# Probability rows in explicitly chosen unit slots, earlier VectorE exponentials, and background matmuls in steps of two, in a fused attention and GLU block

## The chip, the cores and the metric

The kernel runs on one core of one Trainium2 chip. The metric is the device time of one execution in microseconds (us). Executions of one kernel on one chip mostly agree within 1%. "Span" is the length of the profiled execution from its first to its last instruction; it is 1.8 to 2.0 us shorter than the time of the same execution. The profiled execution of the kernel before took 901.75 us, some 4 us less than the median of its runs in the tables, so leads against its profile come out about that much smaller than the differences of medians.

## The reference

One transformer block on 2048 rows of width 512 in bf16: 32 heads of width 16, then a gated MLP of width 1792.

```python
x = A_x                                               # 1 x 2048 x 512
h = x + _A_ref(_layernorm(x), A_wqkv, A_wo)           # softmax attention, 32 heads
h2 = h + _B_ref(_layernorm(h), B_w_gate, B_w_up, B_w_down)
# _A_ref: scores = q k^T * 16**-0.5; p = softmax(scores); o = p v; o @ wo
# _B_ref: (sigmoid(x @ w_gate) * (x @ w_up)) @ w_down
```

The attention makes 32 x 2048 x 2048 exponentials. The kernel cuts them into 2048 **units** of 128 keys x 512 queries of one head (written 128x512 in the profile).

## The kernel before

TensorE makes score tiles in PSUM (transposed: keys on partitions). ScalarE turns most units into fp16 probabilities with `Exp` (`pt`). VectorE makes the others with integer tricks: one instruction per unit from PSUM (`J`), then, for four units together, two bit operations and two products (`X`), which it does in a `chain` of deferred pieces. TensorE multiplies the probabilities with the values into one PSUM accumulator (`acc`), for four heads (a *group*) at a time; at the end of a group VectorE takes `acc` out, and only then the next group's products may start. Normalisation, the Q, K and V projections, the output projection and the MLP of query chunks that are done run as *background* between these.

All order is decided when the program is built: Python keeps a modelled time of each engine (`T["P"]`, `T["A"]`, `T["D"]`) and emits each engine's instructions in the order that the model gives. The pieces that the change touches (cuts are marked `...`):

```python
ptp = main.enter_context(tc.tile_pool(name="ptp", bufs=7))   # 7 tiles of GU = 3 units
NPT = 7

def flush():                     # emit EVERY VectorE and ScalarE job that is ready
    ...
def force(tag):                  # tag: something a score or value matmul needs now
    while After(tag).end is None:
        flush()
        if After(tag).end is None:
            try_bg(1e9, 1e12)

def prep_v(t):                   # one background item: V of 128 keys
    yield pe(4, pm_new)          # ask for room for 4 matmuls at once
    ps = pm_tile()
    v_mm(ps, t)
    done["v", t] = [pm_out(dve(603, lambda: v_out(ps, t), st["mark"]))]

def pt_tile(n):
    if wide["n"] == GU:
        return ptp.tile([P, GU, QC], FP16, name="pt")[:]
    ...                          # early: two-unit places in X, J and 7 "hold" tiles

while n + 1 < len(tiles):        # one exp tile per turn
    ...
    if wide["n"] < GU and not early_on and wide["base"] == 4:   # from 2 to 3 units a tile
        flush()
        wide.update(n=GU, base=2)
    pss_n[n + 1] = scores(n + 1)
    ...
    dable = (len(tl) == GU and tl[-1][:2] not in ((0, 0), (0, 1)) and ...)
    split = (dable and max(T["D"], ...) <= start + 600 and ...)  # last unit to VectorE?
    wa = len(tl) - split
    pt = pt_tile(n)
    ex = nc.scalar.activation(out=pt[:, 0:wa, :], in_=pss[:, 0:wa, :], func=ACT.Exp, scale=AS)
    if split:
        dexp_first(pss[:, GU - 1, :], tl[-1], n)                 # VectorE's J
    ...                          # then background and value matmuls until the exp ends
```

A tile usually gives one of its three units to VectorE, so that seven tiles of three hold about 16 units (in the trace 488 exps from `pt` tiles make two units and 174 make three).

Of the kernel before, what the change touches and what calls it, by code (L numbers as in the profile page):

```python
# [10 lines left out]
FP16 = mybir.dt.float16  # L11
BF16 = mybir.dt.bfloat16
# [131 lines left out]
def kernel(  # L144
# [41 lines left out]
    otp = main.enter_context(tc.tile_pool(name="otp", bufs=6))  # L186
    ptp = main.enter_context(tc.tile_pool(name="ptp", bufs=7))
    dvx = main.enter_context(tc.tile_pool(name="dvx", bufs=1))
# [353 lines left out]
    def prep_v(t):  # L542
        yield pe(4, pm_new)
        ps = pm_tile()
        v_mm(ps, t)
        done["v", t] = [pm_out(dve(603, lambda: v_out(ps, t), st["mark"]))]

    def early_ln(c):
        pr = c
        js = []  # L550
        for i in range(TQ):
            j = None
            if tasks["s", c, i].end is None:
                j = dve(810, lambda i=i: ln_stats(xb[c][:, i, :], mvs[c][:, i, :]), pr=pr)
            elif tasks["f", c, i].end is None:
                j = dve(150, lambda i=i: fix(c, i), pr=pr)
            js.append(j)
        jn = newton_jobs(rstds[c][:], mvs[c][:, :, 1], *js, pr=pr)
        ja = []
        for i in range(TQ):  # L560
            ja.append(dve(325, lambda i=i: apply(c, i), jn, After(("x", c - 1, i // 2)), pr=pr))

        def turn():
            for i in range(0, TQ, 2):
                yield pe(4, pm_new, ja[i], ja[i + 1], ns=8 * 75.0)
                ps = pm_tile()
                pt = ps.bitcast(BF16).rearrange("p (i b q) -> p i b q", i=2, b=DC)
                for k in range(2):
                    for b in range(DC):
                        nc.tensor.transpose(out=pt[:, k, b, :],  # L570
                                            in_=buf["xn", c, i + k][:, b * P:(b + 1) * P],
                                            identity=ident_bf[:])
                pm_out(dve(605, lambda i=i, pt=pt: nc.vector.tensor_copy(
                    out=xnT[c][:, :, i * P:(i + 2) * P].rearrange("p b (i q) -> p i b q", i=2),
                    in_=pt), st["mark"]))
                done["x", c, i // 2] = [st["pms"][-1]]
        return turn()
# [10 lines left out]
    def prep_k(p):  # L588
        for c in range(NQC):
            yield pe(4, pm_new)  # L590
            ps = pm_tile()
            proj8(ps, wk_sb, p, c)
            done["k", p] = [pm_out(dve(603, lambda ps=ps, c=c: nc.vector.tensor_copy(
                out=KT[p][:, c * QC:(c + 1) * QC], in_=ps), st["mark"]))]

    def prep_q(qc, p):
        yield pe(4, pm_new)
        ps = pm_tile()
        proj8(ps, wq_sb, p, qc)
        qd = work.tile([P, QC], BF16, name="qd", bufs=2)  # L600
# [47 lines left out]
    def wo_ln(qc):  # L648
# [5 lines left out]
        for i in range(TQ):  # L654
            yield pe(4, pm_new, otj[qc, NP - 1])
            ps = pm_tile()
            wo_mm(ps, qc, i)

# [26 lines left out]

    def gate_mm(ps, w):
        for d in range(DC):
            nc.tensor.matmul(ps, lhsT=w[:, d, :], rhs=hnT[:, d, :],  # L688
# [34 lines left out]
    def ffn_up(qc, f):  # L723
        yield pe(4, pm_new)
        if f == 0:
# [4 lines left out]
        ps = pm_tile()  # L730
        gate_mm(ps, wgu[:, 0])
        ja = pm_out(act(478, lambda: th.update({f: tanh_out(ps)}), st["mark"]))
        yield pe(4, pm_new)
        ps2 = pm_tile()
        gate_mm(ps2, wgu[:, 1])
        if f % 2:
# [7 lines left out]
    def ffn_down(qc, i):  # L744
        hT, ps = hts[qc], None
        for f in range(0, FC, 4):
            n = min(4, FC - f)
            if f:
# [44 lines left out]
    def try_bg(tokens, loose=60.0, depth=1):  # L793
# [15 lines left out]
        return mm  # L809

    def force(tag):
        while After(tag).end is None:
            flush()
            if After(tag).end is None:
                try_bg(1e9, 1e12)

# [17 lines left out]
    N = ahead // GU  # L834
    wide = {"n": 2, "base": 4}
    STAGES = (150, 225, 360, 530)
# [47 lines left out]
    def scores(n):  # L884
# [4 lines left out]
        pss = PS[:, base:base + wide["n"], :]  # L889
        wide["base"] = {(2, 4): 6, (2, 6): 4, (3, 2): 5, (3, 5): 2}[wide["n"], base]  # L890
        for ui, (qc, g, kt, j) in enumerate(tiles[n]):
# [10 lines left out]
    class Unit:  # L902
        def __init__(self, u, ap, n, end):
            self.u, self.ap, self.n, self.end, self.d = u, ap, n, end, -1

    avq = []
    av_end = {}
    count, todo = {}, {}
    for qc, g in gseq:
        for j in range(4):  # L910
            count[qc, g, j], todo[qc, g, j] = 0, NT
    NPT = 7

    def finish_group(qc, g):
# [52 lines left out]
    def av(limit, loose=60.0):  # L967
# [20 lines left out]
        for un in uns:  # L988
            if un.d < 0:
                av_end[un.n] = T["P"] + DRAIN  # L990
        qc, g = uns[0].u[:2]
# [9 lines left out]
    def dexp_first(src, u, n):  # L1001
# [9 lines left out]
        uns = [Unit(u, None, n, None) for s in range(2)]  # L1011
        for un in uns:
            un.d = 1
        avq.extend(uns)
# [43 lines left out]
    def want_dve(n):  # L1058

        quads[:] = [q for q in quads if any(un in avq for un in q)]  # L1060
        if wide["n"] < GU or not blocks or any(un.n in hold for un in avq):
            return False
# [8 lines left out]

    slots, hold = [], {}

    def early_slots():
        for name, b in (("X", XB), ("J", JB)):
            for i in range(b):
                x = dvx.tile([P, 2, 4, QC] if name == "X" else [P, 4, QC], I16, name=name, bufs=b)
                for s in range(2):
                    slots.extend(([x[:, s, 0:2, :], x[:, s, 2:4, :]]) if name == "X" else [x[:, 2 * s:2 * s + 2, :]])
        slots.extend(prep.tile([P, 2, QC], I16, name=f"hold{i}")[:] for i in range(7))  # L1080

    def pt_tile(n):
        if wide["n"] == GU:
            return ptp.tile([P, GU, QC], FP16, name="pt")[:]
        if not slots:
            early_slots()
        while True:
            busy = {hold[un.n] for un in avq if un.n in hold}
            s = next((s for s in range(len(slots)) if s not in busy), None)
            if s is not None:  # L1090
                break
            flush()
            if not av(8, 1e12):
                try_bg(1e9, 1e12)
        hold[n] = s
        return slots[s].bitcast(FP16)

# [20 lines left out]
    while n + 1 < len(tiles):  # L1118
# [3 lines left out]
        early_on = any(b[1][0] in EARLY for b in bg)  # L1122
        if wide["n"] < GU and not early_on and wide["base"] == 4:
            flush()
            wide.update(n=GU, base=2)
            st["R"] = 1
            N = n + 2 + -(-sum(b.left() for b in blocks) // GU)
        if blocks:
            pss_n[n + 1] = scores(n + 1)
        pss = pss_n.pop(n)  # L1130
        while any(un.n <= n - NPT and un.d < 0 and un.n not in hold for un in avq):
            flush()
            if av(8, 1e12):
                continue
            if half and not chain:
                dexp_rest()
            if not chain:
                break
            pop_chain()
        start = max(T["A"], sc_end[n] + LAT)  # L1140
        if n - NPT not in hold:
            start = max(start, av_end.get(n - NPT, 0.0) + LAT)
        busy = sum(j.ns for j in dq if j.ready() is not None)
        pend = sum(c[0] for c in chain)
        dable = (len(tl) == GU and tl[-1][:2] not in ((0, 0), (0, 1))
                 and not any(un.n in hold for un in avq))
        split = (dable and max(T["D"], sc_end[n] + LAT) <= start + 600 and (half or (len(quads) < XB and len(open_j) < JB))
# [5 lines left out]
        wa = len(tl) - split  # L1153
        pt = pt_tile(n)
        ex = nc.scalar.activation(out=pt[:, 0:wa, :], in_=pss[:, 0:wa, :], func=ACT.Exp, scale=AS)  # L1155
        T["A"] = start + 51 + 426.5 * wa
        ex_end[n] = T["A"] + TAIL["A"]
        avq.extend(Unit(u, pt[:, ui, :], n, ex_end[n]) for ui, u in enumerate(tl[:wa]))
        if split:
            dexp_first(pss[:, GU - 1, :], tl[-1], n)  # L1160
            ex_end[n] = max(ex_end[n], T["D"] + TAIL["D"])
# [24 lines left out]
        if tl[0][0] == NQC - 1 and tiles[n - 1][0][0] < NQC - 1:  # L1186
            nc.sync.dma_start(out=xl[:], in_=x_v[:, (NQC - 1) * TQ:NQC * TQ, :])
        if fw is None and After(("q", 0, NP - 1)).end is not None:
            pre.close()
            fw = main.enter_context(tc.tile_pool(name="fw", bufs=1, reuse_waits="tile"))  # L1190
# [81 lines left out]
    for k, i in enumerate(order):  # L1272
        hn = hnl[i] = ptp.tile([P, GU, QC], FP16, name="pt")[:, 0, :].bitcast(BF16)
        if k % 2 == 0:
# [77 lines left out]
```

## Time and profile before

| | before |
|---|---|
| time, median of 4 runs | 906.2 us (905.28 to 907.01) |
| ScalarE / VectorE / TensorE busy | 86% / 88% / 85% of the span |
| exp units by ScalarE / VectorE | 1561 / 487 |
| first VectorE exp starts | 94.6 us |

The view of busy time by stretches of the kernel before, for the start (17 to 94 us), two parts of the attention and the end. Its columns are the stretch and its length, busy time and number of instructions of TensorE, of TensorE's weight loads, of VectorE (DVE), ScalarE (ACT) and GpSimd, the granted TensorE clock, DMA share and GB/s.

```profile
core 0: us, PE busy (x) PEld busy (x) DVE busy (x) ACT busy (x) POOL busy (x), PEclk, DMA share, GB/s
17.00:94.00 77.00, 57.52 (x396) 19.96 (x397) 39.58 (x102) 57.74 (x54) 0.00 (x0) 0.87 0.08 25
110.00:330.00 220.00, 178.37 (x1393) 50.75 (x1393) 211.83 (x386) 202.91 (x196) 0.00 (x0) 0.91 0.03 8
330.00:800.00 470.00, 423.93 (x3190) 122.01 (x3189) 454.30 (x817) 427.82 (x434) 0.00 (x0) 0.96 0.09 28
840.00:900.00 60.00, 51.18 (x254) 22.09 (x254) 24.82 (x48) 22.02 (x36) 0.00 (x0) 0.95 0.24 74
```

From 330 to 800 us VectorE is 97% busy and ScalarE 91%. At the start VectorE works only half of the time.

ScalarE's waits of the kernel before (who waited for whom; total us, times, longest us). L985 is the value matmul, L893 the score matmul:

```profile
ACT pt L1155 <- PE PS L985: 38.6, 26, 5.2
ACT pt L1155 <- PE PS L893: 19.2, 33, 1.8
ACT th L716 <- PE PS L688: 18.8, 16, 2.1
ACT X L1155 <- PE PS L893: 17.2, 7, 14.4
```

An exp that waits for a *value* matmul doesn't lack input; it lacks a free place to write, since the matmul that still has to read the old contents of its slot has not run. That is 38.6 us. An exp that waits for a *score* matmul lacks input.

The longest slot wait, in the timeline of the kernel before (start, length, engine, line, what; in brackets the idle time before it and who ended it):

```profile
490.80 1.06 PE L893 MATMUL PS<-QT_90,KT_85 32*128 32x512 bf16 x6
491.14 0.54 DVE L674 TENSOR_SCALAR hn<-h,mv,rstd 128x512 bf16<-128x512 f32 x1
...
492.39 0.56 DVE L1033 TENSOR_SCALAR X<-J 128x1536 int16<-128x1536 int16 x1
492.86 1.02 DVE L1043 TENSOR_TENSOR X<-J,X 128x1024 f16<-128x1024 f16 x2
493.00 1.52 PE L985 MATMUL PS<-X,Vaug 128*17 128x512 f16 x6 [1.15 <-DVE X L1033]
494.56 0.72 DVE L940 STREAM_TRANSPOSE xs<-PS 128x512 f32<-128x512 f32 x1 [0.68 <-PE PS L985]
...
495.33 1.03 PE L985 MATMUL PS<-pt,Vaug 128*17 128x512 f16 x8 [0.81 <-DVE xs L940]
...
496.01 4.43 ACT L1155 ACTIVATE pt<-PS 128x1536 f16<-128x1536 f32 x4 [5.16 <-PE PS L985]
```

Read it backwards: ScalarE starts at 496.0 because value matmuls of the next group (495.3) have freed a slot. Those waited for the accumulator's transpose (494.6), this for the last value matmuls of the old group (493.0), and these for VectorE's last `X` pieces (492.4), which stood behind other jobs in VectorE's order. TensorE's scores for the next tiles were done at 491.9, but all seven tiles were full of the next group's probabilities.

The start of the kernel before, in its timeline:

```profile
26.44 0.40 PE L570 MATMUL PS<-ident_bf,xn_336 128*128 128x128 bf16 x4 [0.89 <-DVE xn_336 L328]
...
30.89 0.69 DVE L237 BATCH_NORM_STATS2 st<-xb_111 128x6 f32<-128x512 bf16 x1
...
36.30 0.68 DVE L573 COPY xnT_81<-PS 128x1024 bf16<-128x1024 bf16 x1
...
37.03 1.87 PE L583 MATMUL PS<-xnT_81,w_114 128*128 128x512 bf16 x4 [10.20 <-DVE xnT_81 L573]
...
40.33 1.94 ACT L1155 ACTIVATE X<-PS 128x1024 f16<-128x1024 f32 x2 [14.42 <-PE PS L893]
```

The transposes of key chunk 1 are done at 26.8 us; VectorE copies them out (`xnT_81`) only at 36.3, after statistics of chunk 3 (`xb_111`) that nobody needed yet. ScalarE idles 14.4 us.

### The profile page before, as it was taken

How to read it: one execution, taken by the hardware profiler on the slowest of the kernel's cores; microseconds unless marked ns; L12 is line 12 of the kernel's file. 1: busy time of each engine (PE TensorE's matmuls, PEld its weight loads, DVE VectorE, ACT ScalarE, POOL GpSimd, SP SyncE). 2: the span in 40 equal slices, each digit the busy share in tenths (PEclk: the TensorE clock that was granted, in tenths of full speed). 3: DMA queues.
4: the chain of work that ended last, by engine and by line, in shares of the span. 5: the costliest groups of instructions: out<-in, count | busy, mean ns of one | idle time of the engine just before them, and what ended most of it. 6: DMA issues, size and time to landing. Idle time of an engine off the chain costs nothing.

```text
span 900.0 us, 14693 instructions
## 1 busy us (share of the span) xinstructions
PE 765.6 (85%) x5644; PEld 232.0 (26%) x5644; DVE 795.4 (88%) x1470; ACT 770.8 (86%) x783; POOL 2.9 (0%) x7
## 2 busy tenths in 40 slices
PE   4498888877787899999998989989978898989897
PEld 2132222222222222222222222222222222222343
DVE  7742899999999899999998999999999999899832
ACT  5399998989989999999898999988898998899741
POOL 1000000000000000000000000000000000000000
PEclk9699998899988999999997899999998999899999
DMA  5020002000000001111000001110100101000500
GB/s 198 1 83 1 1 1 59 1 1 2 1 1 1 13 1 47 49 50 33 19 19 1 24 24 48 42 42 13 36 13 1 47 25 34 15 1 13 170 7 27
DMA packets 38219, 26.16 MB, mean 29 GB/s; under 512 B 2560, under 2 KB 38144, under 8 KB 38144
## 3 DMA queue, kind: packets, MB, share of 16 engines
q1 hardware_dynamic: 36512, 23.99, 8.7%
q10 hardware_dynamic: 1632, 1.18, 0.4%
q8 instruction: 46, 0.75, 0.4%
q14 instruction: 29, 0.24, 0.1%
HBM read 23.07 MB, written 2.10 MB: 28 GB/s over the span
## 4 chain that ended last, share of the span: by engine, by line
DVE 37%; ACT 26%; PE 23%; issue 12%; DMA 0%; ACTq 0%; DVEq 0%
ACT pt L1155 23%; DVE J L1007 15%; DVE X L1043 7%; PE PS L688 6%; PE PS L985 5%; PE PS L893 5%; DVE X L1033 4%; DVE X L1038 3%; DVE xs L940 2%; PE PS L264 1%; DVE hT L700 1%; PE PS L1298 1%; PE PS L259 1%; PE PS L705 1%; ACT th L716 1%
## 5 line engine op out<-in xcount | busy, mean ns | idle before, releaser
L1155 ACT ACTIVATE pt<-PS 128x1024 f16<-128x1024 f32 (+1 forms) x663 | 700.8, 1169 | 60.3 <-PE PS L985 38.6
L1007 DVE TENSOR_SCALAR J<-PS 128x512 int16<-128x512 f32 x487 | 324.6, 685 | 16.2 <-PE PS L893 9.1
L985 PE MATMUL PS<-pt,Vaug 128*17 128x512 f16 x1499 | 218.4, 406 | 7.0 <-DVE xs L940 6.8
L1043 DVE TENSOR_TENSOR X<-J,X 128x1024 f16<-128x1024 f16 (+1 forms) x251 | 161.7, 669 | 0.0
L985 PE MATMUL PS<-X,Vaug 128*17 128x512 f16 x1014 | 150.9, 396 | 6.5 <-DVE X L1033 4.7
L985 PEld LDWEIGHTS <-Vaug 128*17 128x17 bf16 x2535 | 63.6, 89 | 151.5 <-issue 130.3
L688 PE MATMUL PS<-xnT_80,wgu 128*128 128x512 bf16 x336 | 89.3, 389 | 1.2 <-DVE hT L700 0.8
L1038 DVE TENSOR_SCALAR X<-J 128x2048 int16<-128x2048 int16 (+3 forms) x133 | 85.3, 642 | 0.2
L1033 DVE TENSOR_SCALAR X<-J 128x2048 int16<-128x2048 int16 (+3 forms) x133 | 85.2, 640 | 0.0
L700 DVE SCALAR_TENSOR_TENSOR hT<-th,PS 128x512 bf16<-128x512 f32 x56 | 38.2, 681 | 18.8 <-PE PS L688 18.8
L716 ACT ACTIVATE th<-PS 128x512 f32<-128x512 f32 x56 | 34.8, 621 | 18.8 <-PE PS L688 18.8
L893 PE MATMUL PS<-QT_90,KT_85 32*128 32x512 bf16 x256 | 39.5, 428 | 12.5 <-ACT pt L1155 12.0
L893 PE MATMUL PS<-QT_93,KT_86 32*128 32x512 bf16 x256 | 37.8, 397 | 10.1 <-ACT pt L1155 9.5
L893 PE MATMUL PS<-QT_92,KT_86 32*128 32x512 bf16 x256 | 37.2, 381 | 10.4 <-ACT pt L1155 9.9
L893 PE MATMUL PS<-QT_91,KT_85 32*128 32x512 bf16 x256 | 36.4, 395 | 11.1 <-ACT pt L1155 10.5
L893 PE MATMUL PS<-QT_94,KT_87 32*128 32x512 bf16 x256 | 35.4, 384 | 11.3 <-ACT pt L1155 11.0
L893 PEld LDWEIGHTS <-KT_84 32*128 32x128 bf16 x512 | 20.5, 91 | 92.0 <-issue 87.3
L705 PE MATMUL PS<-wd,hT 128*128 128x512 bf16 x168 | 43.9, 382 | 0.4 <-DVE ob L710 0.4
L893 PE MATMUL PS<-QT_95,KT_87 32*128 32x512 bf16 x256 | 37.0, 392 | 8.0 <-ACT pt L1155 7.6
L893 PEld LDWEIGHTS <-KT_85 32*128 32x128 bf16 x512 | 20.4, 92 | 89.4 <-issue 88.1
L893 PEld LDWEIGHTS <-KT_86 32*128 32x128 bf16 x512 | 20.2, 91 | 84.7 <-issue 84.4
L893 PEld LDWEIGHTS <-KT_87 32*128 32x128 bf16 x512 | 19.4, 91 | 84.2 <-issue 83.2
(220 smaller groups left out, 531.1 us busy)
## 6 DMA issues: line engine op xcount, KB each, us to landing
wgu<-in_B_w_gate_dram SPq DMA_DIRECT2D x21, 256.0 KB, 2.8
wgu<-in_B_w_up_dram SPq DMA_DIRECT2D x21, 256.0 KB, 3.2
out_dram<-ob SPq DMA_DIRECT2D x16, 128.0 KB, 1.7
wd<-in_B_w_down_dram SPq DMA_DIRECT2D x1, 1792.0 KB, 7.2
xr<-in_A_x_dram SPq DMA_DIRECT2D x12, 128.0 KB, 2.7
X<-in_B_w_gate_dram SPq DMA_DIRECT2D x3, 512.0 KB, 3.9
X<-in_B_w_up_dram SPq DMA_DIRECT2D x3, 512.0 KB, 4.9
wv_sb<-in_A_wqkv_dram SPq DMA_DIRECT2D x1, 512.0 KB, 6.2
```

Source lines behind the costliest of these rows:

```text
L688: nc.tensor.matmul(ps, lhsT=w[:, d, :], rhs=hnT[:, d, :], start=(d == 0), stop=(d == DC - 1))
L700: nc.vector.scalar_tensor_tensor(out=hT[:, f, :], in0=th[:], scalar=1.0, in1=ps, op0=ALU.add, op1=ALU.mult)
L705: nc.tensor.matmul(ps, lhsT=hT[:, f, i * P:(i + 1) * P], rhs=wd[:, f, :], start=(f == 0), stop=(f == FC - 1))
L716: nc.scalar.activation(out=th[:], in_=ps, func=ACT.Tanh, scale=0.5)
L893: mm = nc.tensor.matmul(pss[:, ui, :], lhsT=KT[g // 2][32 * j:32 * j + 32, kt * P:(kt + 1) * P], rhs=q[32 * j:32 * j + 32, :], start=True, ...
L940: j = st["acc"] = dve(650, lambda: nc.vector.transpose(out=xs[:].rearrange("p b r -> p (b r)"), in_=acc), Mark(T["P"] + DRAIN), pr=-1)
L985: nc.tensor.matmul(acc[32 * j:32 * j + VW, :], lhsT=Vaug[:, kt, h, :], rhs=un.ap, start=(c == 0), stop=(todo[qc, g, j] == 0), tile_positio ...
L1007: nc.vector.tensor_scalar(out=J[:, k, :], in0=src, scalar1=ZOFF, scalar2=0.0, op0=ALU.add, op1=ALU.max)
L1033: V.tensor_scalar(out=X[:, 0, 0:k, :], in0=J[:, 0:k, :], scalar1=POWER, scalar2=LITTLE, op0=ALU.bitwise_and, op1=ALU.bitwise_or)
L1038: V.tensor_scalar(out=X[:, 1, 0:k, :], in0=J[:, 0:k, :], scalar1=FRACTION, scalar2=HALF, op0=ALU.bitwise_and, op1=ALU.bitwise_or)
L1043: V.tensor_tensor(out=x, in0=J[:, a:b, :].bitcast(FP16), in1=x, op=ALU.mult)
L1155: ex = nc.scalar.activation(out=pt[:, 0:wa, :], in_=pss[:, 0:wa, :], func=ACT.Exp, scale=AS)
```

## The change

Its intent: (1) probability rows live in unit slots, 36 in one tile and 14 more while the preparation lasts; each exp takes the run of free slots whose last reader is modelled to be done first; (2) `force` emits only the jobs that the wanted result depends on, and normalisation jobs of later chunks come after V's casts; (3) VectorE may take units much earlier; the width of exp tiles goes from 2 to 3 in stages; (4) background matmuls ask for room two at a time. The core of the diff, cuts marked:

```diff
-    ptp = main.enter_context(tc.tile_pool(name="ptp", bufs=7))
+    ptp = main.enter_context(tc.tile_pool(name="ptp", bufs=1))
...
     def prep_v(t):
-        yield pe(4, pm_new)
+        yield pe(2, pm_new, After(("x", t // TQ, t % TQ // 2)))
         ps = pm_tile()
-        v_mm(ps, t)
-        done["v", t] = [pm_out(dve(603, lambda: v_out(ps, t), st["mark"]))]
+        v_mm(ps, t, 0, 2)
+        yield pe(2)
+        v_mm(ps, t, 2, 4)
+        done["v", t] = [pm_out(dve(603, lambda: v_out(ps, t), st["mark"], pr=1))]
...  (the same split for K, Q, the output projection, gate, up and down)
     def early_ln(c):
-        pr = c
+        pr = 2 * (c - 1)
...
+    def place_now(job):
+        if isinstance(job, After):
+            for j in done.get(job.tag, ()):
+                place_now(j)
+        elif isinstance(job, Later):
+            place_now(job.job)
+        elif isinstance(job, Job) and job.end is None:
+            for d in job.deps:
+                place_now(d)
+            if job.ready() is not None:
+                q, e = (dq, "D") if job in dq else (aq, "A")
+                q.remove(job)
+                job.place(e)
+
     def force(tag):
         while After(tag).end is None:
-            flush()
-            if After(tag).end is None:
-                try_bg(1e9, 1e12)
+            place_now(After(tag))
+            if After(tag).end is None and not try_bg(1e9, 1e12):
+                for d in bg[0][2][2]:
+                    place_now(d() if callable(d) else d)
...
+    PLACES = {3: ((4, 2), (6, 2)), 2: ((3, 3), (6, 2)), 1: ((2, 3), (5, 3))}
+    WHEN = {"d": ("k0", 1), 2: ("k0", 2), 1: ("v", NT - 1)}
...
-        if wide["n"] < GU or not blocks or any(un.n in hold for un in avq):
+        if not blocks or not late("d"):
             return False
...
+    NPT, NPE = 36, 14
+    PT = ptp.tile([P, NPT, QC], FP16, name="pt")
+    PE_ = prep.tile([P, NPE, QC], FP16, name="pe")
...
-        dable = (len(tl) == GU and tl[-1][:2] not in ((0, 0), (0, 1))
-                 and not any(un.n in hold for un in avq))
+        dable = len(tl) > 1 and busy <= 1500
...
-        pt = pt_tile(n)
-        ex = nc.scalar.activation(out=pt[:, 0:wa, :], in_=pss[:, 0:wa, :], func=ACT.Exp, scale=AS)
+        free_at, row = p_slots(wa)
+        pt = row[0].tile[:, row[0].i:row[0].i + wa, :]
+        ex = nc.scalar.activation(out=pt, in_=pss[:, 0:wa, :], func=ACT.Exp, scale=AS)
```

## The prediction

> **What bounds the kernel now.** In the middle VectorE and ScalarE share the exponentials, and both are nearly full: the view of busy time by stretches gives, for 300 to 400 us, VectorE 98%, ScalarE 96%, TensorE 90%. Over 100 to 840 us VectorE is idle about 4%, ScalarE about 8%. TensorE has slack: in the list of waits its score matmuls wait 82 us for ScalarE to empty PSUM. One exp unit (128x512) costs ScalarE about 0.46 us, VectorE about 1.35 us (657 us in four groups of lines, 487 units). The middle makes about 2.6 units per us.
>
> Two kinds of time are lost.
>
> 1. The start. The timeline shows ScalarE idle 14.4 us (25.9 to 40.3); it waits for the scores of key chunk 1. VectorE is busy in that gap with statistics and Newton steps of chunks 2 and 3, while the second copy of chunk 1's transposes starts at 36.3, 9.5 us after they ended: `force` flushes every ready job ahead of the needed one. TensorE is idle 10.2 us as well and its clock falls to 0.5, so four dense matmuls take 1.87 us, not 1.04. The Trainium skill ("TensorE: Matmul & The Clock Gate", "What's actually happening") says an idle array runs at half rate; the trace agrees (only 0.5 or 1.0). From 50 to 94 us VectorE is busy 14 to 58%; its first exp comes at 94.6 us.
>
> 2. ScalarE waits for probability slots: 38.6 us in 26 waits for the value matmuls (longest 5.2 us, in a half-clock stretch), I think mostly where one head group ends and the next one's probabilities pile up. Seven tiles hold about 16 units at the usual two per tile.
>
> **What the change does.**
> - `place_now` and the new priorities put only chunk 1's chain on VectorE. By its durations (Newton 2.2 us, four applies 1.3, two copies 1.4, projection 1 to 1.9, cast 0.7) K of chunk 1 is there at 25 to 27 us. The gap shrinks to 0 to 3 us: gain 11 to 13 us, fully critical.
> - VectorE exps from the second chunk on: until about 54 us its fixed work nearly fills it; then some 20 us of idle become about 14 units: gain 4 to 6 us.
> - 36 slots, no longer in threes, hold over twice the units. Slot waits fall from 38.6 us to 5 to 12. Some 28 us of ScalarE are 60 units, over 2.6 per us 23 us; part turns into waits for scores: 12 to 22 us.
> - Steps of two cost TensorE switches: four dense matmuls take 0.97 us from start to next start where 4 x 0.216 is 0.86, so about 0.1 us for each of about 190 split pieces, at most 19 us, against 82 us of slack: off the path, and the next scores come sooner. Net zero to 3 us gained.
> - The last 60 us don't change.
>
> Sum: 27 to 44 us, discounted for overlap. Predicted: 872 us, range 856 to 889. Chances: faster by over 2% 0.83, within 2% 0.15, slower by over 2% 0.02.
>
> **What would show it.** The ScalarE gap near 26 us is under 3 us; the first VectorE exp comes before 60 us; ScalarE's waits for value matmuls total under 15 us; in 100 to 800 us ScalarE is over 94% busy; VectorE makes 495 to 540 units; from the last exp to the end stays near 57 us.
>
> **What would make it wrong.** TensorE becomes the limit (ScalarE's waits for scores rise above the 19 us of now, or more half-clock stretches); early VectorE exps delay V and K casts and stall TensorE; regions of one large tile bring false waits; VectorE at 98% is already the limit.

## The result

| | before | after |
|---|---|---|
| time, median of 4 runs | 906.2 us | 864.65 us (862.06 to 865.35) |
| ratio | | 0.9537 (95%: 0.9514 to 0.9559) |
| ScalarE / VectorE / TensorE busy | 86 / 88 / 85% | 89 / 91 / 88% |
| units by ScalarE / VectorE | 1561 / 487 | 1567 / 481 |
| half-clock time, 110 to 330 us | 41.0 us | 78.5 us |

A ratio is the mean time of one kernel's runs over that of the other kernel's runs of the same rounds, so it isn't quite the ratio of the medians in the tables. Half-clock time is added up from the trace's record of the granted clock, in time from the start of the span (the record begins about 16 us into it).

The stretches of the kernel after (the last one starts where its last exp unit ends):

```profile
core 0: us, PE busy (x) PEld busy (x) DVE busy (x) ACT busy (x) POOL busy (x), PEclk, DMA share, GB/s
17.00:94.00 77.00, 65.03 (x451) 19.96 (x451) 65.83 (x152) 57.64 (x62) 0.00 (x0) 0.91 0.07 25
110.00:330.00 220.00, 179.90 (x1353) 46.73 (x1351) 202.16 (x367) 200.48 (x191) 0.00 (x0) 0.82 0.03 8
330.00:800.00 470.00, 440.40 (x3426) 123.48 (x3424) 459.02 (x828) 462.96 (x466) 0.00 (x0) 0.98 0.10 29
806.00:863.00 57.00, 48.47 (x231) 21.17 (x228) 21.68 (x43) 17.78 (x31) 0.00 (x0) 0.97 0.20 63
```

Three things stand out. From 330 to 800 us ScalarE rose from 427.82 of 470 us (91%) to 462.96 (98.5%). From 110 to 330 us it did not rise at all, and the clock fell from 0.91 to 0.82. And from 17 to 94 us ScalarE was busy about as long as before (57.64 against 57.74 us), although the gap that the change aimed at is closed.

ScalarE's waits of the kernel after (L1016 is now the value matmul, L927 the score matmul):

```profile
ACT pt L1181 <- PE PS L927: 37.2, 35, 9.7
ACT th L724 <- PE PS L696: 14.9, 14, 1.1
...
ACT pt L1181 <- PE PS L1016: 3.8, 3, 1.7
```

The slot waits fell from 38.6 to 3.8 us. The waits for scores total about what they were (19.2 and 17.2 before, 37.2 now), with a new longest of 9.7 us.

The start of the kernel after, in its timeline:

```profile
25.62 1.02 PE L585 MATMUL PS<-xnT_81,w_114 128*128 128x512 bf16 x4 [0.93 <-DVE xnT_81 L575]
...
27.86 9.27 ACT L1181 ACTIVATE pt<-PS 128x1024 f16<-128x1024 f32 x10 [2.78 <-PE PS L927]
...
37.74 0.68 DVE L1038 TENSOR_SCALAR J<-PS 128x512 int16<-128x512 f32 x1
...
46.73 1.33 DVE L1038 TENSOR_SCALAR J<-PS 128x512 int16<-128x512 f32 x2
...
49.04 0.68 DVE L237 BATCH_NORM_STATS2 st<-xb_111 128x6 f32<-128x512 bf16 x1
...
55.70 1.87 PE L585 MATMUL PS<-xnT_83,w_114 128*128 128x512 bf16 x4 [0.78 <-DVE xnT_83 L575]
...
59.05 1.94 ACT L1181 ACTIVATE pt<-PS 128x1536 f16<-128x1536 f32 x2 [9.72 <-PE PS L927]
```

The gap before chunk 1 shrank from 14.4 to 2.8 us. VectorE's first exp starts at 37.7 us. But the last statistics of chunk 3 (`xb_111`) run at 49.0 us, behind VectorE exps (`J`), and ScalarE then idles 9.7 us for the keys of chunk 3. The four matmuls at 55.7 run at half clock (1.87 us instead of 1.02).

To see where time is won I count, in each trace, the exp units that are done (columns of each ScalarE exp / 512, plus one for each `J`), and note when the n-th is reached. This "unit curve" is worked out from the trace's instructions and is used for all runs below. It rests on one profiled execution of each kernel:

| units done | before, us | after, us | lead, us |
|---|---|---|---|
| 32 | 49.7 | 35.3 | 14.4 |
| 64 | 66.6 | 60.5 | 6.1 |
| 192 | 118.6 | 109.7 | 8.9 |
| 512 | 237.8 | 234.2 | 3.6 |
| 1024 | 433.4 | 428.3 | 5.1 |
| 1536 | 640.1 | 619.3 | 20.8 |
| 2048 | 844.1 | 805.9 | 38.3 |
| end of span | 900.0 | 863.3 | 36.7 |

The lead of 14 us at the start is mostly gone at once, and 33 of the 38 us come in the second half of the units.

### The profile page after: what moved, and what is told of

The parts are those of the page before. It is cut to its first block, busy times and chain, and to the rows that moved or that the text cites. A ratio compares the mean times of both kernels' runs of the same rounds, so it can differ in the third digit from the quotient of the medians.

```text
span 863.3 us, 14366 instructions
## 1 busy us (share of the span) xinstructions
PE 759.1 (88%) x5638; PEld 219.8 (25%) x5638; DVE 781.3 (91%) x1450; ACT 768.2 (89%) x783; POOL 2.9 (0%) x7
## 4 chain that ended last, share of the span: by engine, by line
ACT 38%; PE 34%; DVE 19%; issue 8%; DMA 1%; SPq 0%; DVEq 0%; ACTq 0%
ACT pt L1181 35%; PE PS L1016 10%; PE PS L927 9%; PE PS L696 7%; DVE J L1038 7%; DVE X L1072 3%; PE PS L713 2%; DVE X L1062 2%; DVE X L1067 2%; PE PS L1331 1%; DVE hT L708 1%; PE PS L259 1%; ACT th L724 1%; PE PS L264 1%; ACT pe L1181 1%
## 5 line engine op out<-in xcount | busy, mean ns | idle before, releaser
L1181 ACT ACTIVATE pt<-PS 128x1024 f16<-128x1024 f32 (+2 forms) x670 | 706.6, 1184 | 43.2 <-PE PS L927 37.2
L1038 DVE TENSOR_SCALAR J<-PS 128x512 int16<-128x512 f32 x481 | 317.6, 681 | 26.9 <-PE PS L927 19.1
L1016 PE MATMUL PS<-pt,Vaug 128*17 128x512 f16 x1515 | 210.2, 409 | 1.0 <-DVE nt L631 0.3
L1072 DVE TENSOR_TENSOR X<-J,X 128x1024 f16<-128x1024 f16 (+1 forms) x247 | 158.8, 665 | 0.0
L1016 PE MATMUL PS<-X,Vaug 128*17 128x512 f16 x962 | 148.3, 402 | 6.0 <-DVE X L1062 4.1
L696 PE MATMUL PS<-xnT_80,wgu 128*128 128x512 bf16 x336 | 94.0, 384 | 3.2 <-DVE hT L708 2.2
L1016 PEld LDWEIGHTS <-Vaug 128*17 128x17 bf16 x2529 | 60.7, 90 | 139.9 <-issue 118.8
L1067 DVE TENSOR_SCALAR X<-J 128x2048 int16<-128x2048 int16 (+2 forms) x128 | 83.1, 650 | 0.1
L1062 DVE TENSOR_SCALAR X<-J 128x2048 int16<-128x2048 int16 (+2 forms) x128 | 82.9, 647 | 0.0
L927 PE MATMUL PS<-QT_91,KT_85 32*128 32x512 bf16 x256 | 39.7, 437 | 11.1 <-ACT pt L1181 10.6
L927 PE MATMUL PS<-QT_90,KT_85 32*128 32x512 bf16 x256 | 39.4, 434 | 11.0 <-ACT pt L1181 10.6
L713 PE MATMUL PS<-wd,hT 128*128 128x512 bf16 x168 | 47.5, 383 | 0.3 <-DVE ob L718 0.2
L927 PE MATMUL PS<-QT_92,KT_86 32*128 32x512 bf16 x256 | 38.5, 410 | 8.3 <-ACT pt L1181 7.8
L927 PE MATMUL PS<-QT_95,KT_87 32*128 32x512 bf16 x256 | 38.1, 392 | 6.8 <-ACT pt L1181 6.1
L927 PEld LDWEIGHTS <-KT_85 32*128 32x128 bf16 x512 | 19.8, 93 | 93.2 <-issue 91.9
L927 PEld LDWEIGHTS <-KT_84 32*128 32x128 bf16 x512 | 20.2, 91 | 90.7 <-issue 85.0
L927 PE MATMUL PS<-QT_93,KT_86 32*128 32x512 bf16 x256 | 36.6, 394 | 6.8 <-ACT pt L1181 6.3
L927 PEld LDWEIGHTS <-KT_86 32*128 32x128 bf16 x512 | 19.1, 91 | 83.2 <-issue 82.7
L927 PE MATMUL PS<-QT_94,KT_87 32*128 32x512 bf16 x256 | 36.3, 382 | 4.3 <-ACT pt L1181 4.0
L927 PEld LDWEIGHTS <-KT_87 32*128 32x128 bf16 x512 | 19.5, 91 | 79.1 <-issue 78.1
```

What stands on the lines that cost most here:

```text
L696: nc.tensor.matmul(ps, lhsT=w[:, d, :], rhs=hnT[:, d, :], start=(d == 0), stop=(d == DC - 1))
L713: nc.tensor.matmul(ps, lhsT=hT[:, f, i * P:(i + 1) * P], rhs=wd[:, f, :], start=(f == 0), stop=(f == FC - 1))
L927: mm = nc.tensor.matmul(pss[:, ui, :], lhsT=KT[g // 2][32 * j:32 * j + 32, kt * P:(kt + 1) * P], rhs=q[32 * j:32 * j + 32, :], start=True, ...
L1016: nc.tensor.matmul(acc[32 * j:32 * j + VW, :], lhsT=Vaug[:, kt, h, :], rhs=un.ap, start=(c == 0), stop=(todo[qc, g, j] == 0), tile_positio ...
L1038: nc.vector.tensor_scalar(out=J[:, k, :], in0=src, scalar1=ZOFF, scalar2=0.0, op0=ALU.add, op1=ALU.max)
L1062: V.tensor_scalar(out=X[:, 0, 0:k, :], in0=J[:, 0:k, :], scalar1=POWER, scalar2=LITTLE, op0=ALU.bitwise_and, op1=ALU.bitwise_or)
```

## The experiments

Twelve kernels ran, all correct. Their ratios against the kernel before, each measured on the same chip in the same rounds:

| run | what | median, us | ratio (95%) | lead at unit 1024 / 2048, us |
|---|---|---|---|---|
| after | the change | 864.65 | 0.9537 (0.9514 to 0.9559) | 5.1 / 38.3 |
| closed | change + guard (control) | 869.55 | 0.9611 (0.9584 to 0.9638) | 8.9 / 33.5 |
| dlate3 | change, wish for VectorE later | 869.72 | 0.9621 (0.9586 to 0.9656) | 9.0 / 35.3 |
| steps4 | change, steps of four | 879.59 | 0.9723 (0.9687 to 0.9760) | 7.7 / 34.2 |
| slots21 | change, 21 slots | 879.17 | 0.9727 (0.9693 to 0.9761) | 2.9 / 25.0 |
| slots15 | control, 15 slots | 901.20 | 0.9951 (0.9915 to 0.9988) | -4.8 / 3.8 |
| before_pt12 | before, 12 tiles | 867.64 | 0.9603 (0.9569 to 0.9638) | 7.2 / 37.6 |
| before_force | before, forcing by need | 881.66 | 0.9758 (0.9716 to 0.9800) | 3.8 / 21.7 |
| dgate3 | control, VectorE units from chunk 3 | 853.24 | 0.9429 (0.9401 to 0.9458) | 21.7 / 52.5 |
| fill2 | control + useless matmuls | 851.38 | 0.9404 (0.9360 to 0.9449) | 17.0 / 49.1 |
| fill2_dry | fill2's order without them | 861.98 | 0.9550 (0.9507 to 0.9593) | 10.5 / 41.4 |
| gatefill | dgate3 + fill2 | 845.23 | 0.9341 (0.9292 to 0.9389) | 23.6 / 55.9 |
| gatefill_all | the same, fillers everywhere | 839.60 | 0.9293 (0.9245 to 0.9341) | 26.5 / 62.4 |

One caution for reading it: the order is chaotic. `after`, `closed` and `dlate3` differ by edits that should change little, yet they spread from 0.9537 to 0.9621. Differences under about 1% between kernels whose order was reshuffled are not laid to a cause here. The unit curve has scatter of its own: fill2 and fill2_dry (below) give the engines the same work up to the first useless matmul at 140 us, and yet their profiles reach unit 64 at 64.5 and 60.1 us, with 17.1 and 10.2 us of half clock in the first 110 us. Differences of some 4 us between two curves are therefore not read as effects.

### Steps of four in the changed kernel (steps4)

```diff
-        yield pe(2, pm_new)
+        yield pe(4, pm_new)
...  (all seven kinds of background matmul, undone as in the kernel before)
```

> The kernel after with the background matmuls in steps of four again (V, K, Q, output projection, gate, up, down); slots, early units and forcing as in the change. Facts of the two traces: the change's lead over before is 14 us at the 32nd exp unit, 5 us at the 1024th, 38 us at the 2048th, so nearly all is won in the second half, where the FFN's background runs. Theory 1 (deeper slots won the second half): total within 8 us of after (857 to 873 us), lead at unit 2048 over 30 us. Theory 2 (the steps of two won it): 880 us or more, ScalarE's waits for scores in 430 to 800 us come back.

Measured: 879.59 us; lead at unit 2048 34.2 us. Neither theory as put: the exps end only 4 us later than in after (810.0 against 805.9 us), but the end is 11.4 us longer (from unit 2048 to the end of the span 68.8 us, after 57.4, before 55.8). The timeline of TensorE in this run shows why: three down-projection tiles of the MLP were left over when the exps were done and ran alone (after has none of these three there).

```profile
813.75 3.18 PE L705 MATMUL PS<-wd,hT 128*128 128x512 bf16 x14 [1.55 <-DVE hT L700]
817.71 3.18 PE L705 MATMUL PS<-wd,hT 128*128 128x512 bf16 x14 [0.78 <-DVE ob L710]
821.67 3.18 PE L705 MATMUL PS<-wd,hT 128*128 128x512 bf16 x14 [0.78 <-DVE ob L710]
825.33 0.39 PE L1255 MATMUL PS<-xnT,ident 128*128 128x512 bf16 x1
```

So in the changed kernel some 11 us of what the steps of two bring are background work that is not left over. That room for four matmuls at once is found too seldom is the likely reason; it was not counted. In before_pt12 steps of four left far less over (58.7 us from unit 2048 to the end), so this holds for this order, not in general.

### 21 slots in the changed kernel (slots21)

```diff
-    NPT, NPE = 36, 14
+    NPT, NPE = 21, 14
```

> The kernel after with 21 unit slots in the main tile instead of 36 (the bytes of the seven tiles of before; the 14 early slots stay). Theory 1 (depth of the slots): 880 to 900 us, ScalarE again waits over 20 us for value matmuls. Theory 2 (steps of two): 857 to 872 us. A middle result, 870 to 880, would mean that both are needed or that 21 single slots already hold more than seven tiles used at two units each.

Measured: 879.17 us, the middle result; ScalarE waits 22.7 us for value matmuls, where after has 3.8 us:

```profile
ACT pt L1181 <- PE PS L1016: 22.7, 17, 2.6
```

It loses 11 us against after between units 1024 and 2048. Depth matters, but this alone doesn't say how much, since 21 single slots already hold more than 7 tiles at two units each.

### A later wish for VectorE units (dlate3)

```diff
-    WHEN = {"d": ("k0", 1), 2: ("k0", 2), 1: ("v", NT - 1)}
+    WHEN = {"d": ("k0", 3), 2: ("k0", 2), 1: ("v", NT - 1)}
```

> The kernel after with VectorE units allowed from the 4th key chunk on instead of the 2nd. In after's trace the last statistics of chunk 3 run only at 49 us, behind VectorE exps, and ScalarE then idles 9.7 us for that chunk's keys. Theory A (early exps delay the chunk-3 chain): the 9.7 us gap shrinks below 4 us and the total falls by 2 to 8 us against after. Rival B (the gap comes from the order of the normalisation jobs alone): the gap stays above 7 us and the total is the same or up to 4 us longer, since units move from VectorE to ScalarE.

Measured: 869.72 us, gap still 9.73 us. This decides nothing, and the reason is a flaw of the experiment: in its trace VectorE's exps still begin at 39.5 us. `want_dve` only chooses which unit stands last in a tile; whether VectorE takes it is decided by `dable`, which the change freed of any condition on the stage. That reading of the code led to dgate3.

### Twelve tiles in the kernel before (before_pt12)

```diff
-    ptp = main.enter_context(tc.tile_pool(name="ptp", bufs=7))
+    ptp = main.enter_context(tc.tile_pool(name="ptp", bufs=12))
...
-    NPT = 7
+    NPT = 12
```

> The kernel before with 12 probability tiles of three units (36 units) instead of 7, nothing else. Theory 1 (depth of the slots): 870 to 888 us, ScalarE's 38.6 us of waits for value matmuls fall under 12 us. Theory 2 (steps of two): the slot waits fall too but turn into waits for scores, 893 to 906 us.

Measured: 867.64 us, ratio 0.9603. Theory 1 holds, and the run is 2.4 us faster than its range: two changed numbers in the program give 36.5 us (medians 904.1 and 867.64). ScalarE's waits in this run (the last line has the slot waits):

```profile
ACT X L1155 <- PE PS L893: 17.2, 7, 14.4
ACT th L716 <- PE PS L688: 14.7, 13, 1.1
ACT pt L1155 <- PE PS L893: 13.9, 30, 1.8
...
ACT pt L1155 <- PE PS L985: 4.3, 3, 1.7
```

The slot waits did not turn into waits for scores: those fell too, from 19.2 to 13.9 us. The 14.4 us gap at the start is still there; the lead is -0.8 us at unit 192, 7.2 us at 1024 and 37.6 us at 2048. Busy time moved as a slot story wants it: from 330 to 800 us ScalarE rose from 427.82 to 461.19 us. The Trainium skill ("Perfetto Trace Analysis", "Optimization Strategy") says that consistent bubbles on the engine that should be saturated can mean that there isn't enough SBUF or PSUM for the next tile; this agrees, with 26 such bubbles of 38.6 us cut to 3 of 4.3 us by buffer count alone.

### The control (closed)

While I prepared variants with another order, some were refused before any run, because a PSUM bank was read in the middle of an accumulation: with steps of two, another background item can begin between the halves of one, or the number of banks can change there. The control adds a guard:

```diff
+            if oi is not None and bg[i] is not oi:      # a half-done tile goes first
+                continue
...
-        if st["R"] > 1 and wide["i"] == 0 and late(st["R"] - 1):
+        if st["R"] > 1 and wide["i"] == 0 and not st["open"] and late(st["R"] - 1):
```

> Control. The kernel after with a guard only: while a background tile has had two of its four matmuls, no other background tile is begun, and the number of banks is not changed. Variants of the change with another order of work were refused without it (a bank was read in the middle of an accumulation). It changes a few positions in the order. Expected: after's time within the scatter that a reshuffled order brings, 860 to 872 us, same unit curve within 4 us; the next three runs are compared with this one.

Measured: 869.55 us, within what was expected. It is the measure for the next runs.

### Fifteen slots (slots15)

```diff
-    NPT, NPE = 36, 14
+    NPT, NPE = 15, 14
```

> The control with 15 unit slots in the main tile, which is what seven tiles hold at two units each, so before's effective depth, with all else of the change kept. Theory 1 (depth of the slots carries the gain, 36.5 us in the run of the kernel before with twelve tiles): 888 to 905 us, ScalarE's waits for value matmuls 30 us or more. Theory 2 (early units, forcing and steps of two carry a good half): 875 to 887 us. With 21 slots it was 879 us.

Measured: 901.20 us, ratio 0.9951, in theory 1's range. With fifteen slots all other parts of the change together are worth 0.5%. ScalarE's waits in this run (L1025 is the value matmul):

```profile
ACT pt L1190 <- PE PS L1025: 56.8, 35, 5.7
ACT pt L1190 <- PE PS L936: 18.9, 23, 3.5
```

But the slot waits are 56.8 us, against 38.6 in before and 22.7 with 21 slots: by this measure fifteen single slots hold less than the seven tiles, and 21 hold more. So what the rest is worth at before's depth should lie between 0.5% and the 2.7% of slots21; it isn't shown more exactly, and one part of it alone gives 2.4% in before_force, the next run.

Together with before_pt12 this settles the main point: depth alone, without the rest, gives 0.9603; the rest, without added depth, should lie between 0.9951 and 0.9727; with both it is 0.9537 to 0.9611. The gains don't add: once there is depth, the rest brings little more (0.9603 against 0.9537 to 0.9611).

### Forcing by need alone (before_force)

```diff
(the kernel before, and of the change only:)
+    def place_now(job): ...      # and the new force, as in the diff above
-        pr = c
+        pr = 2 * (c - 1)
...
-        yield pe(4, pm_new)
+        yield pe(4, pm_new, After(("x", t // TQ, t % TQ // 2)))      # V; K and Q likewise
...
-        done["v", t] = [pm_out(dve(603, lambda: v_out(ps, t), st["mark"]))]
+        done["v", t] = [pm_out(dve(603, lambda: v_out(ps, t), st["mark"], pr=1))]
```

> The kernel before with only the forcing by need (place_now), the new priorities of normalisation jobs and V casts, and the dependences that these need; no early VectorE units, seven tiles, steps of four. Prediction's term: the gap of 14.4 us before chunk 1 falls to 0 to 3 us and 11 to 13 us are gained at the end. Theory K (the lead is kept, as dgate3's 8 us at unit 96 was nearly kept to the end): 892 to 897 us. Rival G (given back, because the gap only moves to a later chunk or seven tiles swallow it): lead at unit 64 under 6 us or lost by unit 1024, total 899 to 906 us.

Measured: 881.66 us, ratio 0.9758. Better than either theory. The lead is 11.2 us at unit 64, falls to 3.8 us at unit 1024 (so far G is right: it isn't kept), and then rises to 21.7 us at 2048. The second rise was expected by nobody. The slot waits are 32.0 us, little less than 38.6; half-clock time from 330 to 800 us is 17.1 us, against 41.0 in before. Whether the clock, the changed order (the caution above) or forcing in the later groups makes it is open. (The 8 us at unit 96 in the expectation are 9.5 us in the unit curve below.) It overlaps with depth: 22 us and 36 us alone, 36 to 42 us together (closed and after).

### VectorE units really gated (dgate3)

```diff
-    WHEN = {"d": ("k0", 1), 2: ("k0", 2), 1: ("v", NT - 1)}
+    WHEN = {"d": ("k0", 3), 2: ("k0", 2), 1: ("v", NT - 1)}
...
-        dable = len(tl) > 1 and busy <= 1500
+        dable = len(tl) > 1 and busy <= 1500 and late("d")
```

> The control with the VectorE share of an exp tile really forbidden until K of chunk 3 is placed (the run dlate3 gated only the wish for a VectorE unit, and VectorE units still began at 40 us, so it decided nothing). Theory A (early exps delay the chunk-3 chain): the 9.7 us gap of ScalarE before chunk 3 falls below 4 us, first VectorE exp after 45 us, unit 96 is reached at least 2 us sooner. Rival B (order of the normalisation jobs): the gap stays above 7 us. What is left of it at the end tells whether an early lead is kept: if half-clock stretches between 110 and 330 us set the pace there, the total moves under 3 us.

Measured: 853.24 us, ratio 0.9429, 16 us under the control on the same chip. The chain of chunk 3, in this run's timeline of VectorE:

```profile
38.21 0.68 DVE L237 BATCH_NORM_STATS2 st<-xb 128x6 f32<-128x512 bf16 x1
...
49.82 0.69 DVE L577 COPY xnT<-PS 128x1024 bf16<-128x1024 bf16 x1 [1.04 <-PE PS L574]
51.63 0.69 DVE L589 CAST KT<-PS 128x512 bf16<-128x512 f32 x1 [1.11 <-PE PS L587]
52.87 1.29 DVE L1047 TENSOR_SCALAR J<-PS 128x512 int16<-128x512 f32 x2 [0.55 <-PE PS L936]
```

The last statistics run at 38.2 us instead of 48.7 in the control, the keys are there at 52.3 instead of 58.0, ScalarE's longest wait from 20 to 100 us is 2.85 us, and the clock is never halved in the first 110 us (13.7 us in the control). Theory A holds. Unit 96 is reached 9.5 us sooner than in the control, and this lead is kept: 12.8 us at unit 1024, 19.0 us at 2048. So it was wrong to think that an early lead is lost in the middle whatever happens; that hypothesis of mine falls. What belongs to the gate by its chain is the 9.5 us at unit 96 (6.9 us in gatefill, which has the same gate); why the lead then doubled (the half-clock time from 110 to 330 us is 54.6 us against 64.9, and the order changed) was not tested.

### Useless matmuls in the idle places of TensorE (fill2)

```diff
+            if (70 <= n < 270 and st["R"] == 1 and st["fill"] < n and not st["open"]
+                    and T["P"] + 400 <= lim):
+                last_pm = pm_new()
+                if last_pm is None or (last_pm.end is not None and last_pm.end + LAT <= T["P"]):
+                    for _ in range(2):
+                        nc.tensor.matmul(PS[:, 1, :], lhsT=ident_bf[:], rhs=xnT[2][:, 0, :], start=True, stop=True)
+                    pe_time("dense", MM * 2)
...
```

> The control with up to two useless dense 128x512 matmuls per tile into the spare PSUM bank where the schedule leaves TensorE idle, tiles 70 to 270 only (about 110 to 330 us, where dense background work is nearly absent and the clock was halved 78 us in after, 44 us in before). Theory H (TensorE idle makes the clock halve, and the half clock starves ScalarE there): half-clock time in 110 to 330 us falls under 40 us and unit 1024 is reached 5 to 12 us sooner than in the control, the total 4 to 12 us shorter. Rival (clock isn't what holds that stretch, or fillers cost as much as they give): unit 1024 within 2 us or later.

(The 78 and 44 us in this text were read with the clock record's own zero, which lies 11 us before the span. In span time they are 78.5 and 41.0 us, and the control has 64.9 us.)

Measured: 851.38 us, ratio 0.9404; half-clock time from 110 to 330 us 6.8 us; unit 1024 at 416.4 us, the control at 424.5. The total is 18 us under the control, more than the 4 to 12 us expected. The stretches of this run:

```profile
110.00:330.00 220.00, 208.21 (x1594) 57.23 (x1595) 214.82 (x390) 214.28 (x208) 0.00 (x0) 0.98 0.04 10
330.00:800.00 470.00, 438.24 (x3409) 125.44 (x3402) 458.63 (x825) 456.89 (x459) 0.00 (x0) 0.98 0.11 33
```

### The same order without the useless matmuls (fill2_dry)

```diff
-                    for _ in range(2):
-                        nc.tensor.matmul(PS[:, 1, :], lhsT=ident_bf[:], rhs=xnT[2][:, 0, :], start=True, stop=True)
                     pe_time("dense", MM * 2)
```

> The schedule of fill2 with the useless matmuls left out: the scheduler counts their time but nothing is issued, so the order of all other work is that of fill2. Theory H (the fillers keep the clock up, and that is the gain): half-clock time in 110 to 330 us back above 40 us, total 860 to 874 us like the control. Rival R (the reshuffled order is the gain): 848 to 856 us like fill2, whatever the clock.

Measured: 861.98 us, ratio 0.9550, half-clock time from 110 to 330 us 58.0 us. Its stretches:

```profile
110.00:330.00 220.00, 183.26 (x1378) 49.33 (x1387) 206.63 (x374) 204.54 (x198) 0.00 (x0) 0.87 0.03 8
330.00:800.00 470.00, 434.33 (x3360) 125.07 (x3410) 458.50 (x823) 459.50 (x462) 0.00 (x0) 0.97 0.10 29
```

The order of all useful work is the same in these two (in the traces ScalarE's 783 and VectorE's 1447 instructions and all weight loads of useful matmuls stand in the same order), so the difference in the first line is the fillers': 138 of them, counted in the two programs, raise the clock from 0.87 to 0.98 and ScalarE from 204.54 to 214.28 of 220 us. From unit 192 to unit 1024 fill2 takes 302.6 us (113.8 to 416.4), fill2_dry 312.8 (110.1 to 422.9). Theory H holds. Of fill2's 2.1% against the control some 1.5% (0.9550 to 0.9404) is the clock, and the rest may be the reshuffle.

The Trainium skill ("TensorE: Matmul & The Clock Gate", "Why this matters for your kernels") advises to have no TensorE idle gaps over about 3 us between bursts. That is not enough here: in after the longest idle stretch of TensorE between 110 and 330 us, worked out from the trace's matmul times, is 0.96 us, and still the clock was halved for over a third of that time. The same page's "A second HAM failure mode" fits better: it tells of a kernel whose frequent micro-idles make the clock swing.

### Both, and fillers everywhere (gatefill, gatefill_all)

```diff
(dgate3's two lines and fill2's fillers; gatefill_all also:)
-            if (70 <= n < 270 and st["R"] == 1 and st["fill"] < n and not st["open"]
+            if (30 <= n < 2000 and st["R"] == 1 and st["fill"] < n and not st["open"]
```

> dgate3 and fill2 together: VectorE units from K of chunk 3 on, fillers in tiles 70 to 270. If the two gains are of different causes they add: dgate3 was 14 us and fill2 16 us (by ratio, 0.018 and 0.021) under the control, so 834 to 844 us. If not, near 850 us.

(By the medians dgate3 and fill2 were 16 and 18 us under the control; the ratios in this text are right.)

Measured: 845.23 us, ratio 0.9341, just above the expected range: the two gains add in part (0.0182 and 0.0207 alone, 0.0270 together).

> As gatefill with fillers allowed from tile 30 to the end of the attention. Theory H says that the half-clock time left after unit 1024 (about 30 us in dgate3, 17 us in fill2) goes too: 828 to 842 us, half clock outside the start and the tail under 10 us. Rival: late in the kernel TensorE is over 94% busy, fillers find few places or delay scores: same as gatefill within 4 us or slower.

Measured: 839.60 us, ratio 0.9293. The granted clock of this run in 40 slices, from its page:

```profile
PEclk9999999999999999999999999999999999999999
```

In the page of the kernel after it reads:

```profile
PEclk9969998777898769999999699999998999999999
```

Half-clock time is 13.6 us in the whole span (after: 116.5), and 10.2 us between 110 us and the last exp, just over the 10 us expected. This is the fastest version, 7% under the kernel before, and it computes the right result. It is within the two intervals' reach of gatefill, so the fillers outside tiles 70 to 270 aren't shown to pay by themselves.

## Why the prediction was right or wrong

The time was predicted at 872 us with a range of 856 to 889; it is 864.65. The sum was nearly right, with terms that were not, and that they cancelled was luck: the slots were counted with 12 to 22 us and give 36.5 alone, while of the 15 to 19 us counted for the start 5.5 us were left at unit 96.

- **The slots: right mechanism, size too small.** Predicted 12 to 22 us of the sum; twelve tiles alone give 36.5 us. Two factors were off. I converted 28 us of ScalarE into 23 us of time and then took off more because "part turns into waits for scores". The slot waits fell to 3.8 us (predicted 5 to 12), and in before_pt12 the waits for scores and for the MLP's gate matmuls fell as well, from 19.2 to 13.9 and from 18.8 to 14.7 us. In the changed kernel, from 100 us to the last exp, the waits for scores are 20.6 us against 18.8 before: nearly unchanged.
- **The cause of the slot waits**, that the next group's probabilities pile up at a group's end: right for most. In 19 of the 26 waits, 34.0 of the 38.6 us, the old group's accumulator is taken out during the wait.
- **The gap before chunk 1: right about the gap, wrong about the gain.** It fell to 2.78 us (predicted 0 to 3), keys at 27.4 us (predicted 25 to 27). But "gain 11 to 13 us, fully critical" failed: at unit 64 the lead was 6.1 us. The step that failed is the assumption that the freed VectorE time is free for chunk 3's chain. The first VectorE exp came at 37.7 us, not after 54, and delayed the statistics of chunk 3; a new gap of 9.7 us appeared. dgate3 shows it: without those exps the gap goes and unit 96 comes 9.5 us sooner (16 us in all, of which the later part has no tested cause).
- **VectorE exps from the second chunk on: "gain 4 to 6 us" was not had in the start.** The exps before chunk 3's keys cost more than they gave (dgate3 against the control); those after 54 us, on which the estimate rested, were not tested alone. VectorE made 27 units before 94.6 us, where it made none before. VectorE was busy 65.83 instead of 39.58 us from 17 to 94 us, ScalarE 57.64 instead of 57.74. The prediction named this among its dangers ("early VectorE exps delay V and K casts and stall TensorE").
- **The lead did not grow in the middle**: 8.9 us at unit 192 and 5.1 us at unit 1024, a difference within the scatter of the curves, although slots were free. Half-clock time from 110 to 330 us rose from 41.0 to 78.5 us, a danger that was named too. fill2 against fill2_dry shows that half-clock time costs: about 0.2 us per us (10.2 us of 51.2). By that, as an estimate from one profile of each of these two runs, 37.5 us more cost some 7.5 us. Why the changed order has more half-clock time than before is not shown.
- **Steps of two: "net zero to 3 us gained" was too small** for this order: steps4 lost 15 us of median, 11.4 of them as background left over at the end. What the extra switches cost was not measured apart.
- **What should show:** slot waits under 15 us, right; ScalarE over 94% busy in 100 to 800 us, right on the whole (96%), but only 91% from 110 to 330; the end near 57 us, right (57.4); VectorE with 495 to 540 units, wrong (481): it made more at the start (27) and fewer after 330 us (308 against 331). That ScalarE took more because it no longer waited fits before_pt12, where with the slots alone VectorE made 465.

What stays open: what the rest of the change is worth at exactly before's depth, the 18 us that forcing by need brings in the second half of before_force, and how much of the spread among after, closed and dlate3 is order alone.

## What to carry to other kernels

When a consumer that works in a fixed order stops at a group's end, the depth of the buffer in front of it decides whether the producer stops too; look for producers that wait for a *reader*, and try the buffer count alone before rebuilding anything. Closing one gap only pays if the next chain behind it has its turn: freed time of a shared engine goes to whatever the scheduler offers first, so gate optional work behind the chain that is needed next. And where TensorE waits for other engines, look at the granted clock before asking it for less work.

## What the Trainium skill lacked or had wrong

- "TensorE: Matmul & The Clock Gate" ("Why this matters for your kernels", "HAM oscillation"): the rule of no idle gaps over about 3 us did not keep the clock up here. With no idle stretch over 0.96 us (110 to 330 us of after) and TensorE 82% busy by the profile (179.90 of 220 us), the clock was halved for 78.5 of 220 us. A rule in terms of how much array work a window holds is lacking. The two states of its table, half and full clock, are the only ones in these traces (0.5 and 1.0).
- The same page says to keep TensorE busy, but not with what when the useful work leaves only short gaps. 138 useless 128x512 matmuls in idle places cut half-clock time from 58.0 to 6.8 us (110 to 330 us) and the time by about 1.5% (ratios 0.9550 and 0.9404).
- "Perfetto Trace Analysis" ("Optimization Strategy") says that consistent bubbles can mean too few buffers, and, just before, to find the instruction that ends a wait; it doesn't join the two. Here a lack of buffers was told from a lack of input by who ended the wait: a reader of the old contents (38.6 us) or the maker of the input (19.2 us).
- None of the pages I used says how far a changed order of instructions moves a time: three nearly equal kernels spread from 0.9537 to 0.9621 of the kernel before.
